# Copying mask factors on GpSimd, turning inputs earlier and moving two transform steps to another PSUM bank, in a fused block-sparse attention and Fourier-mixing kernel

## The chip, the cores and the metric

The kernel runs on one core of a Trainium2 chip. The metric is the device time of one execution in microseconds (us), lower is better. All times below are medians of runs in the fast state. Engines are written PE (TensorE, matrix products), PEld (its weight loads), DVE (VectorE), ACT (ScalarE), POOL (GpSimd) and SP (SyncE, which issues DMAs). "L580" is line 580 of the kernel.

## The reference, cut to what matters

Attention over 4 batches and 8 heads with a block mask, then a Fourier mixing block with a channel network. All is float32.

```python
# q, k, v: (4, 8, 768, 64); blocks of 32; mask: neighbours, first and last block, 3 random blocks a row
scores = scale * q @ k^T;  scores = where(mask, scores, -1e9)
attn = softmax(scores);    o = attn @ v
x = o.transpose(0, 2, 1, 3).reshape(4, 768, 512)
mixed = real(fft(fft(x, axis=1), axis=2))
u = x + mixed
un = (u - mean(u)) / sqrt(var(u) + 1e-6)            # "whitened"
out = u + relu(un @ w_ch1) @ w_ch2                  # 512 -> 2048 -> 512
```

## The kernel before

Two heads of one batch make a pair; there are 16 pairs. A pair has 6 slots, so a batch has SB = 24, and a slot computes the scores, exponentials and values of 2 units (128 keys by 384 queries for both heads). The Fourier and channel work of one batch, its "mixer", is woven in behind the attention of the next batch. The weaving is done while the kernel is built: each engine has a modelled clock `when`, each PSUM bank a modelled time `free`, and `gap` emits mixer work while the model says that it fits. On the chip every engine then works through its own list in that fixed order, so the place of an instruction in the list matters as much as its duration.

Some names of tiles: `s` and `e` are scores and their exponentials; `oT` and `xt` carry the output of the attention into `x`. The others in the profiles belong to the mixer: `sa` and `sd` to its folds (sums and differences of rows before the transform), `zp` and `zs` to the transform's later steps, `un`, `utp` and `unT` to the whitened tiles, and `xp`, `yp`, `z` and `y` are its products.

The mask of the first batches can be added by the matrix unit, through two bf16 factors (L580). They lie in buffers that later serve the running sums of the exponentials, so they are copied away in slot 19:

```python
    def keep_factors():                                    # called when sl == SB - 5
        kept = room(2, [P, 2, S], "factors", BF16)         # the room of a weight chunk
        for a, t in enumerate(factors["at"]):
            nc.sync.dma_start(out=kept[:, a, :], in_=t)    # L479
        factors["at"] = kept[:, 0, :], kept[:, 1, :]       # all later units read the copy
```

From the fifth pair on, keys and queries of the next pair are turned by VectorE in blocks of 32 (`flip_blocks`, L537) and put in order by ScalarE (`in_order`, L545); `squares` takes a sum of squares for a range check. The order within a slot, cut:

```python
        got = scores(units)                                # PE: L570, and L580 for the mask
        for u, ps in got:
            weigh(u, ps)                                   # ACT: exponential; DVE: mask, where PE didn't add it
        if not paired and not late:
            gap(1.5)                                       # mixer work that fits, such as the folds
        while due and (opens or not paired):
            sum_up()                                       # values (PE L633), and sums (DVE L614 or POOL L619)
        ...                                                # more mixer work, channel steps, copies
        if BY_VECTOR <= n + 1 < len(pairs):                # the turns, at the end of the slot
            for at, fn, args in ((0, squares, (n + 1, 0)), (1, flip_blocks, (n + 1, 0)),
                                 (2, in_order, (n + 1,)), (4, flip_blocks, (n + 1, 1)),
                                 (5, squares, (n + 1, 1))):
                if s == at:
                    fn(*args)
```

The sums of a pair close in `total`, which reads both halves of the summed exponentials, `acc`, and frees their buffers:

```python
    def total(n):
        sp, at = ps_t.tile([P, HS], FP32, tag="t", name="sp"), bank("t")
        for half in range(2):
            acc = acc_of.pop((n, half))
            for i in range(2):
                ...
                nc.tensor.matmul(sp[g:g + BLK, :], ..., acc[:, i, :], ...)      # L715
```

PSUM has one bank "t" and two banks "m" for small steps. The third step of the transform, `along(2)`, took both "m" banks (`side` and `zp`), and the last whitened tile was turned over (`un_flip(1, 1)`, L958) through an "m" bank. An "m" bank is also where the products of the mixer want to go.

## Time and profile before

| | before |
|---|---|
| median (lowest to highest) | 1080.43 (1079.89 to 1081.24), 4 runs |
| span of the profiled execution | 1079.5 |
| PE busy | 1042.1 |
| PE idle | 37.4 |
| longest waits of PE | 9.2 for the copied factors, 4.5 for the turned keys |

A line of the timeline has the start, the time taken, the engine, the kernel's line, the operation, the output and the inputs with their shapes, and a count when equal instructions were put together; the bracket at the end is idle time of that engine just before, and who ended it. The prediction shows the main lines. These, from the timeline of the kernel before, matter later. They are two of the last folds in VectorE's list before the sum at 166.66, and the next sum of GpSimd:

```profile
165.65 0.56 DVE L788 TENSOR_TENSOR sa<-sa 128x384 f32<-128x384 f32 x1
166.13 0.29 DVE L787 TENSOR_TENSOR e<-e 128x128 f32<-128x128 f32 x1
...
171.43 1.00 POOL L619 TENSOR_TENSOR acc<-e 128x384 f32<-128x384 f32 x1 [7.69 <-ACT e L590]
```

GpSimd starts the next pair's sums at 171.43, a microsecond after L715 has begun at 170.42, and so after the folds.

### The profile page before, as it was taken

Reading aid. Unit: us, or ns where it says so; the run is one execution under the profiler, and the core shown is the slowest. Engines: PE = TensorE matmul, PEld = TensorE weight load, DVE = VectorE, ACT = ScalarE, POOL = GpSimd, SP = SyncE. Lnnn points to the kernel's source line nnn. Section 1 sums busy time; section 2 is a strip of 40 time slices with the busy share of each in tenths; the row PEclk is TensorE's granted clock in tenths of the full one; section 3 lists DMA queues with packets and bytes.
Section 4 is the critical chain, followed back from the end, with each engine's and each line's share of the span. In section 5 each row is a group of like instructions: output and inputs, shape, how many; then the busy total and the mean of one; then the engine's idle time right before and its main releaser. Section 6 shows DMA issues by size and latency. Waiting matters only on the chain.

```text
span 1079.5 us, 12378 instructions
## 1 busy us (share of the span) xinstructions
PE 1042.1 (97%) x4378; PEld 537.1 (50%) x4378; DVE 661.5 (61%) x1226; ACT 376.4 (35%) x742; POOL 227.4 (21%) x256
## 2 busy tenths in 40 slices
PE   8999789999999999999999999999999999999996
PEld 4433234444455545444444555444444555568575
DVE  5899494777763634764568446665557255675663
ACT  5998555564311202443451302343320212210210
POOL 1000062323600001265454000354630001000000
PEclk9999899999999999999999999999999999999998
DMA  7757222221000001222211000212000001000001
GB/s 224 220 177 239 69 45 44 45 45 30 15 0 1 1 0 30 59 39 42 52 29 31 1 0 18 64 29 39 14 9 7 0 1 30 29 1 1 1 19 43
DMA packets 120769, 47.04 MB, mean 44 GB/s; under 512 B 108142, under 2 KB 113532, under 8 KB 120700
## 3 DMA queue, kind: packets, MB, share of 16 engines
q1 hardware_dynamic: 118812, 45.38, 17.1%
q10 hardware_dynamic: 1856, 0.79, 0.3%
q8 instruction: 36, 0.59, 0.2%
q14 instruction: 33, 0.27, 0.1%
q0 software_dynamic: 32, 0.01, 0.0%
HBM read 37.11 MB, written 6.29 MB: 40 GB/s over the span
## 4 chain that ended last, share of the span: by engine, by line
PE 90%; DVE 6%; issue 2%; ACT 1%; DMA 0%; POOL 0%; SPq 0%; ACTq 0%; POOLq 0%; DVEq 0%
PE y L1089 23%; PE z L1033 15%; PE s L570 12%; PE o L633 11%; PE yp L1033 8%; PE yy L1152 6%; PE xp L1033 4%; PE zp L843 2%; PE sp L701 1%; PE s L580 1%; PE zp L814 1%; PE tp L503 1%; PE utp L958 1%; PE sp L715 1%; PE xt L657 1%
## 5 line engine op out<-in xcount | busy, mean ns | idle before, releaser
L619 POOL TENSOR_TENSOR acc<-acc,e 128x384 f32<-128x384 f32 x154 | 156.8, 1055 | 212.2 <-ACT e L590 137.6
L570 PE MATMUL s<-qT,kT 64*128 64x384 f32 x768 | 154.3, 517 | 7.7 <-DVE kT L537 4.5
L633 PE MATMUL o<-e,vr 128*64 128x384 f32 x768 | 142.8, 500 | 0.0
L1092 DVE TENSOR_TENSOR x<-y,x 128x512 f32<-128x512 f32 x72 | 49.7, 690 | 133.1 <-PE y L1089 133.0
L1089 PE MATMUL y<-w_sb,hA 128*128 128x512 f32 x288 | 129.3, 596 | 1.7 <-ACT zs L845 1.7
L1089 PE MATMUL y<-w_sb,hB 128*128 128x512 f32 x288 | 128.5, 596 | 1.0 <-DVE x L1092 1.0
L595 DVE TENSOR_TENSOR e<-s,mask 128x768 f32<-128x768 f32 x98 | 89.0, 950 | 54.2 <-ACT s L593 48.5
L570 PEld LDWEIGHTS s<-qT,kT 64*128 64x128 f32 x768 | 64.6, 187 | 82.8 <-issue 26.1
L593 ACT ACTIVATE s<-s 128x768 f32<-128x768 f32 x98 | 74.3, 791 | 84.2 <-PE s L570 83.9
L1033 PE MATMUL z<-unT,t 128*128 128x384 f32 x256 | 93.2, 487 | 0.3 <-DVE hA L1038 0.3
L1089 PEld LDWEIGHTS y<-w_sb,hB 128*128 128x128 f32 x288 | 53.4, 190 | 67.7 <-issue 65.3
L590 ACT ACTIVATE e<-s 128x768 f32<-128x768 f32 x94 | 71.2, 812 | 42.6 <-PE s L580 38.6
L1089 PEld LDWEIGHTS y<-w_sb,hA 128*128 128x128 f32 x288 | 53.0, 190 | 65.5 <-issue 58.8
L906 POOL TENSOR_SCALAR st<-st 128x1 f32<-128x1 f32 x24 | 8.3, 348 | 358.8 <-DVE st L905 358.8
L633 PEld LDWEIGHTS o<-e,vr 128*64 128x64 f32 x768 | 48.3, 137 | 71.0 <-issue 67.6
L1038 DVE TENSOR_TENSOR hA<-z,hA 128x384 f32<-128x384 f32 x64 | 35.7, 557 | 77.8 <-PE z L1033 77.8
L1042 ACT ACTIVATE hA<-hA 128x384 f32<-128x384 f32 x64 | 33.4, 523 | 120.4 <-DVE hA L1038 120.3
L619 POOL TENSOR_TENSOR acc<-e 128x384 f32<-128x384 f32 x40 | 42.9, 1094 | 111.9 <-PE sp L715 85.7
L1033 PEld LDWEIGHTS z<-unT,t 128*128 128x128 f32 x256 | 48.5, 190 | 34.7 <-DVE hA L1038 1.3
L1042 ACT ACTIVATE hB<-hB 128x384 f32<-128x384 f32 x64 | 33.5, 523 | 85.9 <-DVE hB L1038 85.9
L1053 ACT COPY hA<-xp 128x384 f32<-128x384 f32 x32 | 15.3, 479 | 113.0 <-PE xp L1033 113.0
L1033 PE MATMUL xp<-unT,w_sb 128*128 128x384 f32 x128 | 47.6, 494 | 2.6 <-DVE x L1092 2.6
(204 smaller groups left out, 1430.8 us busy)
## 6 DMA issues: line engine op xcount, KB each, us to landing
wraw<-in_moe_w_ch_dram SPq DMA_DIRECT2D x32, 512.0 KB
vr<-in_v_dram SPq DMA_DIRECT2D x30, 192.0 KB
qb<-in_q_dram SPq DMA_DIRECT2D x44, 96.0 KB
kb<-in_k_dram SPq DMA_DIRECT2D x44, 96.0 KB
x<-oT SPq DMA_DIRECT2D x192, 12.0 KB
out_dram<-x SPq DMA_DIRECT2D x16, 128.0 KB
out_dram<-x SPq DMA_DIRECT2D x8, 256.0 KB
qr<-in_q_dram SPq DMA_DIRECT2D x24, 64.0 KB
```

Source lines behind the costliest of these rows:

```text
L570: nc.tensor.matmul(s[:, i, 0:HS], kT[rows, c * P:(c + 1) * P], qT[rows, queries], start=True, stop=u not in by_pe)
L590: nc.scalar.activation(out=e, in_=s[:, :, 0:HS], func=ACT.Exp, scale=scale)
L593: nc.scalar.activation(out=s[:, :, 0:HS], in_=s[:, :, 0:HS], func=ACT.Exp, scale=scale)
L595: nc.vector.tensor_tensor(out=e, in0=s[:, :, 0:HS], in1=m.broadcast_to([P, 2, HS]), op=ALU.mult)
L619: nc.gpsimd.tensor_add(out=acc[:, i, :], in0=start[:, i, :], in1=e[:, i, :])
L633: nc.tensor.matmul(o[D * i:D * i + D, :], vt[:, i, c, :], e[:, i, :], start=(c == 0), stop=(c == C - 1))
L1033: nc.tensor.matmul(to, a[:, k, :], c[:, k, :], start=(k == 0), stop=(k == ND // 2 - 1))
L1038: tt(out=to, in0=ps, in1=a, op=ALU.add)
L1042: nc.scalar.activation(out=h, in_=h, func=ACT.Relu)
L1089: nc.tensor.matmul(y, hs[0, half][:, l, m * P:(m + 1) * P], w2_sb[:, 4 * r + l, :], start=(l == 0), stop=(l == 3))
L1092: nc.vector.tensor_tensor(out=x[:, m, :], in0=y, in1=x[:, m, :], op=ALU.add)
L1152: nc.tensor.matmul(ps, a[:, k, :], c[k // 2][:, k % 2, :] if isinstance(c, list) else c[:, k, :], start=(k == 0), stop=(k == 3))
```

## The change

It has three intentions: GpSimd copies the factors in place of two DMAs; the turns stand right behind the exponentials of their slot, so that the turned keys are there earlier; the transform's third step and the last whitened tile use the turns' bank "t", so that an "m" bank is left for products. The diff without its bookkeeping for the model:

```diff
-            nc.sync.dma_start(out=kept[:, a, :], in_=t)
+            nc.gpsimd.tensor_copy(out=kept[:, a, :], in_=t)
...
-                side = ps_m.tile([P, 512], FP32, tag="m", name="side")
-                at = bank("m")
+                side, at = ps_t.tile([P, 512], FP32, tag="t", name="side"), bank("t")
...
-        first += [("M" if g == 2 else "m", lambda g=g: along(g), 2.1, (1.0 if g < 2 else 0.5), 0.0)
+        first += [("mt" if g == 2 else "m", lambda g=g: along(g), 2.1, (1.0 if g < 2 else 0.5), 0.0)
...
-            tag, pool = (("t", ps_t), ("m", ps_m))[half]
+            tag, pool = (("t", ps_t), ("m", ps_m))[half == 1 and m != 1]
...
         for u, ps in got:
             weigh(u, ps)
+        if BY_VECTOR <= n + 1 < len(pairs):
+            for at, fn, args in ((0, squares, (n + 1, 0)), (1, flip_blocks, (n + 1, 0)),
+                                 (2, in_order, (n + 1,)), (4, flip_blocks, (n + 1, 1)),
+                                 (5, squares, (n + 1, 1))):
+                if s == at:
+                    fn(*args)
         if not paired and not late:
             gap(1.5)
...
-        if BY_VECTOR <= n + 1 < len(pairs):
-            ...                                   (the same lines, at the end of the slot)
```

I call the three parts A (the copy), B (the turns) and C (the banks).

More of the change, by code (lines that the diff above doesn't have):

```diff
@@ L1194, in outputs @@
             ahead(4)
-        fl = [[("tm"[h], lambda h=h, m=m: un_flip(h, m), 0.6, 0.55, 0.0) for m in range(T)]
+        fl = [[("tm"[h == 1 and m != 1], lambda h=h, m=m: un_flip(h, m), 0.6, 0.55, 0.0)
+               for m in range(T)]
               for h in range(2)]
@@ L1252, in do_apart @@
         if kind != "-":
-            at = bank(kind.lower())
+            at = bank(kind[0])
             done = busy("PE", pe, done) + HOP
@@ L1279, in gap @@
             elif kind != "-":
-                bank_at = (max if kind == "M" else min)(free[kind.lower()])
-                if kind.lower() in used or max(state["ready"], bank_at) > when["PE"] + 0.1:
+                bank_at = max(min(free[k]) for k in kind)
+                if (any(k in used for k in kind) or
+                        max(state["ready"], bank_at) > when["PE"] + 0.1):
                     break
-                used += kind.lower()
+                used += kind
             do_apart()
@@ L1444, in slot @@
             item[2]()
-        if BY_VECTOR <= n + 1 < len(pairs):
-            for at, fn, args in ((0, squares, (n + 1, 0)), (1, flip_blocks, (n + 1, 0)),
-                                 (2, in_order, (n + 1,)), (4, flip_blocks, (n + 1, 1)),
-                                 (5, squares, (n + 1, 1))):
-                if s == at:
-                    fn(*args)
         w_loads()
```

## The prediction

> **What bounds the kernel now.** I read the page first, then the list of waits of TensorE, then the timeline around the long ones, then a table of stretches for the clock. To order the timeline by the program I also had the unchanged program print the order in which it emits its work; no time comes from that.
>
> The page and the waits of TensorE (who waited for whom, us in total, times, longest):
>
> ```profile
> span 1079.5 us, 12378 instructions
> PE 1042.1 (97%) x4378; PEld 537.1 (50%) x4378; DVE 661.5 (61%) x1226; ACT 376.4 (35%) x742; POOL 227.4 (21%) x256
> ...
> PE s L580 <- DMA factors<-at_q: 9.2, 1, 9.2
> PE s L570 <- DVE kT L537: 4.5, 1, 4.5
> ...
> PE xp L1033 <- DVE x L1092: 2.6, 3, 1.8
> PE y L1089 <- ACT zs L845: 1.7, 3, 0.6
> PE s L570 <- DVE e L595: 1.6, 2, 0.8
> ```
>
> TensorE is busy 97%, so only its idle time, 1079.5 - 1042.1 = 37.4 us, and any time at a low clock can be won. The change adds no matmul and takes none away. The five waits shown are 19.6 of the 37.4 us, and each of the three parts of the change aims at some of them.
>
> The timeline at the first wait (start, duration, engine, line):
>
> ```profile
> 110.17 0.69 DVE L462 TENSOR_TENSOR w_sb<-w_sb,wraw 128x512 f32<-128x512 f32 x1
> 110.92 0.53 SPq L479 DMA_DIRECT2D factors<-at_k  x1
> 111.50 0.60 SPq L479 DMA_DIRECT2D factors<-at_q  x1
> ...
> 115.64 0.82 PE L580 MATMUL s<-factors 64*128 64x384 bf16 x4 [9.16 <-DMA factors<-at_q]
> ```
>
> The copies can't start before 110.86, when VectorE has finished with the weight chunk in whose buffer the copy goes (110.17 + 0.69). The transfer is only the last 115.64 - 110.86 = 4.8 us of the 9.16; the rest is that buffer.
>
> At the second wait:
>
> ```profile
> 154.10 2.54 DVE L766 TENSOR_TENSOR sa<-x 128x1536 f32<-128x1536 f32 x1
> ...
> 160.71 1.49 DVE L537 STREAM_TRANSPOSE kT<-kb 128x768 f32<-128x768 f32 x1
> ...
> 162.35 2.93 PE L570 MATMUL s<-qT,kT 64*128 64x384 f32 x8 [4.53 <-DVE kT L537]
> ...
> 166.66 0.95 DVE L614 TENSOR_TENSOR acc<-acc,e 128x768 f32<-128x768 f32 x1
> ...
> 170.42 0.85 PE L715 MATMUL sp<-acc,pick 128*32 128x384 f32 x8
> ```
>
> The turn of the keys stands behind three folds in VectorE's queue (at 154.10, 156.57 and 159.05), and VectorE has no gap from 147.09 to 168.75. Eight score matmuls that take 1.5 us elsewhere took 2.93 here. The table of stretches (us, PE busy and count, the other engines, granted clock, DMA share, GB/s) says why:
>
> ```profile
> 115.60:120.50 4.90, 4.86 (x20) 1.10 (x19) 0.00 (x0) 1.51 (x2) 0.00 (x0) 0.50 0.00 0
> ...
> 162.30:165.00 2.70, 2.65 (x8) 1.47 (x10) 2.66 (x4) 0.87 (x2) 1.43 (x2) 0.50 0.26 42
> ```
>
> After both long waits the clock is halved: 4.86 us of work behind the first and 2.65 behind the second cost half of that, 2.4 and 1.3 us. So the first wait costs 9.2 + 2.4 = 11.6, the second 4.5 + 1.3 = 5.8 us.
>
> **What the Trainium skill says.**
> - "TensorE: Matmul & The Clock Gate", "What's actually happening": an idle window of about 3.4 us halves the clock, and a busy one of the same length restores it. The trace agrees: both low stretches follow idle times over 3.4 us, and no shorter wait has one.
> - "GPSIMD Engine Reference", "4.1 Engine selection": one-input operations run near line rate on GpSimd, two-input ones about twice as slow as on VectorE; "3.1 Elementwise" gives about 2.6 cycles an element for two inputs and 1.03 to 1.8 for short loops. The kernel has no GpSimd copy; its additions of 384 columns take 1055 ns in the mean, 0.98 when undisturbed, which agrees with 2.6 cycles.
> - "DMA: Bandwidth & Descriptors", "Anatomy of one DMA": some 2 us fixed plus the size over the bandwidth, so about 2.5 us for 192 KB. Here the second transfer took 4.1 us from its issue (111.50) to its use (115.64): slower, behind earlier loads.
> - "SBUF — State Buffer", "SBUF: two separate sides": VectorE instructions with two SBUF inputs and GpSimd exclude each other. It agrees: L614 takes 1.76 us at 152.42 beside GpSimd's sums and 0.95 alone. The new copies run at 110.9, when VectorE is idle until 123.8, so they meet nobody.
>
> **Part 1, the copy by GpSimd.** Removed: two DMAs. Added: two one-input copies of 128x768. Estimate from the GPSIMD page: 768 x 1.03 to 1.8 cycles at 1.2 GHz is 0.66 to 1.15 us, plus some 0.15 us each, so 1.6 to 2.6 us for both, which start at 110.9 as the DMAs do. TensorE goes on at 112.6 to 113.6, I take 113.0: 2.6 us earlier. The idle time is still 6.5 us, so the clock still falls. With the low windows where they lie now (steps of 3.41 us, one ending at 117.1, the next at 120.5) the low stretch is 113.0 to 117.1 in place of 115.6 to 120.5: 0.4 us less loss. Gain 3.0 us. From there to 147 no other wait of TensorE is over 0.4 us, so it is kept.
>
> **Part 2, the turns.** Nothing is added or removed; the turn of the keys moves in front of the three folds that the same slot emits. It then runs from about 154.2 to 155.7 (its data landed before 144, by the DMA packets), and TensorE needs it at 157.8. Taken alone this wins the whole 5.8 us. But the sum of VectorE's work up to L614 at 166.66 is the same, and that addition closes the sums that L715 reads. TensorE stands in order: scores of the slot from 157.85, next slot's scores, values up to about 165, then L715, which can't start before 167.61 + 0.1. Now it starts at 170.42. So I keep 2.7 us, and about 2.7 us of new idle time appear in front of L715. That is shorter than a window, so I count no lower clock. Further, squaring the keys now comes directly behind the exponentials of its own slot and no longer holds up the exponentials of the next one, which is what the timeline shows before the 0.78 us wait at 258.88: 0.7 us. In all other slots the order on ScalarE and VectorE hardly changes. Gain 3.4 us.
>
> **Part 3, the banks.** The transform's third step took both "m" banks, and the next y product waited for a copy out of one (0.57 us, three times): 1.7 us gained. The last whitened tile leaves its "m" bank, so the first product of the next quad need not wait for L1092. But two of these three waits won't vanish: at 444 and 694 the "t" bank holds the softmax sums, which VectorE takes out at 444.75 and 696.01, when L1092 is nearly done as well. So only the last (0.35 us) counts, and I subtract 0.5 us for a stall on "t" behind the sums. Gain 1.5 us.
>
> Sum: 3.0 + 3.4 + 1.5 = 7.9 us; 1080.5 - 7.9 = 1072.6.
>
> **Rivals.**
> (a) VectorE's chain does not bind and the turn's whole cost is won: another 3 us, 1069.5. For it: the order of folds and sums may change, since the emission follows a model of busy times. Against: VectorE has no gap from 147 to 168.75.
> (b) The new wait in front of L715 is long enough to halve the clock, and GpSimd's copy is slow (2 us each, as two-input ones would be): the first part wins about 1 us and the second about 1.5: some 1076.
> (c) The earlier turns and the shared "t" bank disturb the later batches, where exponentials, masks and quads stand close: each lost 0.5 us, in three batches, some 1075. Against it: in paired slots the turn was emitted close behind the exponentials already.
> (d) The buffer of the weight chunk comes free later because something else on VectorE comes first. Against: nothing before 110 changes.
>
> **Range and chances.** I predict 1072.5 us. Part 1 may be 1 us off either way, part 2 from 1 to 6, part 3 from -1 to 3; together some 4 us each way: 1068.5 to 1077. Two per cent are 21.6 us; all waits that the change can reach, with their clock loss, are 11.6 + 5.8 + 5.9 = 23.3 us, so faster by over 2% needs nearly all of them gone: 1%. Slower by over 2% would need a new wait of 22 us: 1%.
>
> **What would show it.** Step 1: two GpSimd copies of 0.8 to 1.3 us from 110.9, the wait at L580 about 6.5 us, still a low clock behind it. Step 2: no wait of scores for kT; a wait of some 2.7 us in front of L715 for L614, near 162 to 165. Step 3: no wait of y for zs. It is wrong if the copies take over 2 us, if TensorE does not wait at L715 and the time falls below 1069, or if a wait for exponentials, masks or the "t" bank grows by over 2 us.

## The result, and the profile after

| | before | after |
|---|---|---|
| median (lowest to highest), 4 runs each | 1080.43 (1079.89 to 1081.24) | 1077.72 (1076.34 to 1078.51) |
| ratio, with its 95% interval | | 0.9973 (0.9956 to 0.9990) |
| span of the profiled execution | 1079.5 | 1075.9 |

A ratio is the mean time of one kernel's fast runs over that of the other's fast runs of the same rounds, so it isn't quite the ratio of the medians. By the rule of 2% the kernels are the same. The gain is 2.7 us where I had predicted 7.9, and the time lies 0.7 us above my range.

The page of the kernel after:

```profile
span 1075.9 us, 12388 instructions
...
PE 1042.7 (97%) x4378; PEld 536.5 (50%) x4378; DVE 665.4 (62%) x1226; ACT 375.7 (35%) x742; POOL 231.1 (21%) x258
```

PE's idle time fell from 37.4 to 33.2 us, and its busy time grew by 0.6 us although it has the same 4378 products. So some of them ran longer; a table below shows where the clock was lower. The waits of PE after (who waited for whom; us in total, times, longest):

```profile
PE s L580 <- POOL factors L479: 6.1, 1, 6.1
PE sp L715 <- DVE acc L614: 3.8, 1, 3.8
...
PE xt L657 <- ACT unT L958: 2.0, 1, 2.0
```

The wait for the factors shrank from 9.2 to 6.1, the waits for turned keys (4.5) and for `zs` (1.7) are gone, and the two longest new ones are at L715 and L657. To see what each stretch gained I set the start of the same slot's first score product against itself in both traces:

| slots | after minus before, us | what is there |
|---|---|---|
| 0 to 20 | -0.3 | nothing changed: scatter |
| 20 to 22 | -3.4 | the factors |
| 22 to 30 | -4.0 | the wait for turned keys (-4.5), a new one of 0.5 |
| 30 to 36 | +6.0 | the new wait at L715 (3.8), and more work at a low clock behind it than before |
| 36 to 42 | 0.0 | |
| 42 to 54 | +1.5 | the new wait at L657, less what the banks gain there |
| 54 to 60 | +0.5 | the banks: two new waits, 0.2 and 0.5, for one of 0.4 |
| 60 to 84 | -1.6 | the banks |
| 84 to the last product | -1.8 | the banks |
| behind the last product | -0.5 | |

The sum is -3.6, the difference of the spans. Three of these rows deserve their lines. First the factors, in the timeline after:

```profile
110.68 0.82 POOL L479 COPY factors<-at_k 128x768 bf16<-128x768 bf16 x1 [105.58 <-DVE w_sb L462]
111.45 0.83 POOL L479 COPY factors<-at_q 128x768 bf16<-128x768 bf16 x1
112.33 0.82 PE L580 MATMUL s<-factors 64*128 64x384 bf16 x4 [6.15 <-POOL factors L479]
```

GpSimd had nothing to do for 105.58 us; it waited for VectorE to leave the weight chunk in whose room the copy goes. Both copies together are over in 1.6 us, but the wait is still 6.15 us, because most of it is that room.

Then the sums, about 50 us later, in the timeline after:

```profile
150.96 1.54 DVE L537 STREAM_TRANSPOSE kT<-kb 128x768 f32<-128x768 f32 x1
...
161.33 0.84 PE L715 MATMUL sp<-acc,pick 128*32 128x384 f32 x4
162.34 2.27 POOL L619 TENSOR_TENSOR acc<-e 128x384 f32<-128x384 f32 x2 [1.73 <-ACT e L590]
162.53 1.23 DVE L788 TENSOR_TENSOR sa<-sa 128x384 f32<-128x384 f32 x1
163.69 1.08 DVE L787 TENSOR_TENSOR e<-e 128x128 f32<-128x128 f32 x1
...
165.01 0.95 DVE L614 TENSOR_TENSOR acc<-acc,e 128x768 f32<-128x768 f32 x1
166.01 1.50 PE L715 MATMUL sp<-acc,pick 128*32 128x384 f32 x4 [3.84 <-DVE acc L614]
```

Read it from the bottom. The second half of L715 waited 3.84 us for the sum of 165.01. That sum is late because two folds before it took 1.23 and 1.08 us, where they took 0.56 and 0.29 before. They took longer because GpSimd's sum lies right beside them, from 162.34. And that sum could start because the first half of L715 had run at 161.33 and given back its buffer: before, all eight products of L715 came together, after the folds. (The bracket of GpSimd's sum names the exponentials, which came last; that it needs the buffer too is shown by e4.)

The table of stretches after (start:end, us, then PE, PEld, DVE, ACT and POOL busy with counts, granted clock, DMA share, GB/s) shows what the new wait does to the clock:

```profile
161.40:164.80 3.40, 0.77 (x5) 0.07 (x4) 3.33 (x5) 0.06 (x1) 2.27 (x2) 0.99 0.00 0
164.80:171.50 6.70, 5.49 (x17) 2.19 (x18) 5.40 (x9) 1.50 (x2) 0.00 (x0) 0.50 0.01 2
```

PE worked 5.49 us at half the clock there; if half of it is loss, that is 2.7 us. In the kernel before, PE worked 3.18 us at half the clock behind the wait for turned keys (162.12 to 165.53), by the same estimate a loss of 1.6 us.

Last the wait at L657, in the timeline after:

```profile
230.86 1.88 ACT L545 COPY qT<-qb 128x256 f32<-128x256 f32 x6
232.65 0.58 ACT L958 COPY unT<-utp 128x512 f32<-128x512 f32 x1
233.28 0.55 PE L657 MATMUL xt<-ident,oT 128*128 128x128 f32 x3 [1.99 <-ACT unT L958]
```

and the same step of the kernel before:

```profile
232.68 0.59 ACT L959 COPY unT<-utp 128x512 f32<-128x512 f32 x1
233.15 1.92 ACT L545 COPY qT<-qb 128x256 f32<-128x256 f32 x6
```

The two ScalarE entries have changed places. The copy to `unT` empties bank "t", of which there is only one, and L657 needs that bank; so six small copies of `in_order`, 1.88 us, now stand between PE and its bank.

### The profile page after: what moved, and what is told of

It reads as the page before. It is cut to its first block, busy times and chain, and to the rows that moved or that the text cites. A ratio compares the mean times of both kernels' runs of the same rounds, so it can differ in the third digit from the quotient of the medians.

```text
span 1075.9 us, 12388 instructions
## 1 busy us (share of the span) xinstructions
PE 1042.7 (97%) x4378; PEld 536.5 (50%) x4378; DVE 665.4 (62%) x1226; ACT 375.7 (35%) x742; POOL 231.1 (21%) x258
## 4 chain that ended last, share of the span: by engine, by line
PE 88%; DVE 7%; ACT 2%; issue 2%; POOL 1%; DMA 0%; ACTq 0%; DVEq 0%; POOLq 0%
PE y L1088 22%; PE z L1032 15%; PE s L570 12%; PE o L633 10%; PE yp L1032 7%; PE yy L1151 6%; PE xp L1032 4%; PE zp L842 2%; PE sp L701 1%; PE s L580 1%; PE zp L814 1%; PE utp L957 1%; DVE x L743 1%; PE sp L715 1%; PE tp L503 1%
## 5 line engine op out<-in xcount | busy, mean ns | idle before, releaser
L619 POOL TENSOR_TENSOR acc<-acc,e 128x384 f32<-128x384 f32 x150 | 152.1, 1050 | 85.3 <-DVE e L595 83.2
L619 POOL TENSOR_TENSOR acc<-e 128x384 f32<-128x384 f32 x44 | 48.2, 1115 | 127.1 <-PE sp L715 93.6
L1032 PE MATMUL z<-t,w_sb 128*128 128x384 f32 x128 | 46.7, 488 | 0.9 <-DVE t L994 0.9
```

The source lines that it names most:

```text
L619: nc.gpsimd.tensor_add(out=acc[:, i, :], in0=start[:, i, :], in1=e[:, i, :])
L1032: nc.tensor.matmul(to, a[:, k, :], c[:, k, :], start=(k == 0), stop=(k == ND // 2 - 1))
```

## The experiments

**My theory.** A does what I predicted. B removes the wait for keys, but gives that back at L715, where the chain of VectorE also gets longer through the collision with GpSimd and the clock halves; and it loses some 2 us more by `in_order` in front of the copy that empties bank "t". C gains more than I had counted. **The rivals.** (1) The parts disturb each other, and none of them alone loses. (2) The loss after slot 42 belongs to C, which puts more work through bank "t". (3) The long wait at L715 is merely VectorE's sum of work, and the collision has no part in it.

All twelve runs gave correct results, in the fast state. They came in three calls, on three chips, and each is given as a ratio to the kernel before on the same chip, whose medians were 1080.89, 1080.67 and 1080.65 us. All ratios lie within 2% of 1, so all of them are "same" by that rule; the intervals tell them apart.

### e1: the copy alone

The kernel before, with A:

```diff
-            nc.sync.dma_start(out=kept[:, a, :], in_=t)
+            nc.gpsimd.tensor_copy(out=kept[:, a, :], in_=t)
```

> The kernel before with the GpSimd copy alone. Theory (the ledger of the two traces): the wait for the factors goes from 9.2 to 6.1 us and the low clock behind it from some 4.9 to some 4 us of work, 3.4 us in all, and nothing else changes: 1077.1 us, the wait for kT stays at 4.5 us. Rival: an earlier first stage is eaten by the chain of VectorE before kT, whose wait then grows: 1080, wait for kT over 6 us.

Measured: 1077.63 us (1076.85 to 1078.02, 6 runs), ratio 0.9969 (0.9956 to 0.9981), which is 3.3 us gained. The wait for the factors is 6.2 us and the wait for keys still 4.5. The theory holds for A.

### e2: the turns alone

The kernel before, with the block of five turn steps moved to behind `weigh`, as in the change.

> The kernel before with the earlier turns alone. Theory: the wait for kT (4.5 us and 1.3 us of low clock) is replaced by a wait of 3.8 us in front of L715, longer than a clock window of 3.4 us, so the clock is halved again and some 2.8 us are lost: no gain, 1080 to 1083 us. Rival (my prediction's second step): the wait in front of L715 is 2.7 us, without a low clock behind it: 1077 us.

Measured: 1084.35 us (1083.64 to 1085.25, 6 runs), ratio 1.0033 (1.0020 to 1.0045): 3.5 us lost, more than I had expected, since that left out L657. Its waits of PE:

```profile
PE sp L715 <- DVE acc L614: 3.8, 1, 3.8
...
PE xt L657 <- ACT unT L959: 2.0, 1, 2.0
```

Both new waits are there without A and C. The clock was 0.50 from 166.0 to 172.8, as long as after the whole change. Rival 1 falls: a part that I had credited with 3.4 us costs 3.5.

### e3: the banks alone

The kernel before, with C.

> The kernel before with the two changes of banks alone. Theory: the waits of y for zs (1.7 us) and of xp for L1092 (2.6 us) go, two short ones on the t bank and for L994 come (0.7 each), so 2.8 us are won after 430 us: 1077.7 us if the 1.5 us that the changed kernel lost between 221 and 430 us belong to the turns, 1079.2 us if they belong to the banks (a new wait of L657 for L958 near 233 us would show it). Rival (prediction's third step): 1.5 us won, 1079.

Measured: 1076.48 us (1075.19 to 1078.25, 5 runs), ratio 0.9959 (0.9945 to 0.9973): 4.4 us gained, where I had expected 3.2, or 1.7 if the wait at L657 belonged to the banks. The waits for `zs` (1.7 us) and for `un` at the products `yp` (0.5) are gone; the three waits of `xp`, 2.6 us, are replaced by 0.5 at L957 (bank "t"), 1.0 at the products `z` and 0.35 at a product `y`. Two of these in its list of waits:

```profile
PE z L1032 <- DVE t L994: 1.0, 2, 0.5
...
PE utp L957 <- DVE sums L683: 0.5, 2, 0.2
```

From slot 36 to the last product PE's idle time is 3.0 us less and the time 4.1 us less. There is no wait at L657, and slots 42 to 54, which lost 2.3 us in e2, gain 1.3 us here. Rival 2 falls.

### e4: the halves of the total reversed

The kernel after, with the late half of L715 first, so that no buffer comes free before the folds are over:

```diff
-        for half in range(2):
+        for half in (1, 0):
```

> The changed kernel with the two halves of the sum in L715 in reversed order: its first four matmuls then wait for L614, so the sums' first buffer stays taken and GpSimd can't start the next pair's sums at 162.3 us, beside VectorE's folds. Theory: L788 and L787 go back from 1.23 and 1.08 us to 0.56 and 0.29, L614 ends 1.5 us earlier, the wait in front of L715 is 2.4 to 2.9 us (four matmuls more stand behind it), under a clock window, and no low clock follows: 1074 to 1075 us. Rival: the wait grew from 2.7 to 3.8 us because the turn of the keys or a different order made VectorE's chain longer; then the wait stays near 3.8 to 4.3 us with the low clock: 1077.5 to 1078.5 us.

Measured: 1075.59 us (1073.94 to 1075.81, 5 runs), ratio 0.9947 (0.9933 to 0.9960), 2.8 us better than the change. Its timeline:

```profile
162.64 0.56 DVE L788 TENSOR_TENSOR sa<-sa 128x384 f32<-128x384 f32 x1
163.11 0.28 DVE L787 TENSOR_TENSOR e<-e 128x128 f32<-128x128 f32 x1
163.64 0.95 DVE L614 TENSOR_TENSOR acc<-acc,e 128x768 f32<-128x768 f32 x1
164.65 1.36 PE L715 MATMUL sp<-acc,pick 128*32 128x384 f32 x8 [3.14 <-DVE acc L614]
166.15 2.18 POOL L619 TENSOR_TENSOR acc<-e 128x384 f32<-128x384 f32 x2 [5.42 <-PE sp L715]
```

The folds are back at 0.56 and 0.28 us, and the last sum starts at 163.64 instead of 165.01, 1.4 us earlier. Rival 3 falls: the collision cost that much. In slots 30 to 36 this kernel needs 2.4 us less than the change. The wait gives 0.7 of them. The other 1.7 us are PE's busy time: 3.41 us of work at half clock in place of 5.54, and the eight products of L715 together in 1.36 us, where the two separate halves took 0.84 and 1.50. Yet I missed two things. The wait is 3.14 us where I had expected 2.4 to 2.9, since the early half of L715 no longer fills a part of it. And I had expected no low clock behind it, but one of 3.4 us came, although the wait was shorter than a step of the clock. What makes the clock fall was thus open; e7, e9 and e10 bear on it.

### e5: the copy and the banks, without the turns

> The changed kernel without the earlier turns (copy and banks). Theory: the parts add up (3.3 for the copy, 4.4 for the banks, -3.5 for the turns in the runs of them alone), so this is faster than the changed kernel: 1073.2 us, with the kT wait of 4.5 us still in it. Rival: the parts overlap, and without the turns the changed kernel loses: 1077 to 1080 us.

Measured: 1074.47 us (1073.17 to 1075.17, 5 runs), ratio 0.9941 (0.9928 to 0.9955), a gain of 6.2 us. Against the change's 0.9973 that is 3.5 us better: B costs the same beside A and C as alone. A and C together are 1.5 us less than 3.3 + 4.4 us, within the intervals of the two. The traces show where such scatter can come from: behind the unchanged wait for keys the low clock lasted 6.8 us here and 3.4 us before, because the steps of the clock fell otherwise.

### e6: the turn of the keys alone

The kernel before, with only the turn of the keys moved:

```diff
         for u, ps in got:
             weigh(u, ps)
+        if BY_VECTOR <= n + 1 < len(pairs) and s == 4:
+            flip_blocks(n + 1, 1)
...
-                                 (2, in_order, (n + 1,)), (4, flip_blocks, (n + 1, 1)),
-                                 (5, squares, (n + 1, 1))):
+                                 (2, in_order, (n + 1,)), (5, squares, (n + 1, 1))):
```

> The kernel before with one of the five moved steps alone, the turn of the keys; squares, the queries' turn and its ordering stay at the end of the slot. Theory: the swap of the kT wait for the L715 wait (3.3 to 3.8 us and a low clock of up to 6.8 us) is here, so it gains nothing: 1081 to 1082.5 us; but the 2.3 us that the turns alone lost between 221 and 430 us are not, since they come from the ordering of the queries (1.9 us on ScalarE) queued in front of the copy L959 that frees the t bank. So it is 2 to 3 us faster than the turns alone (1084.35), and no wait of L657 for L959 is seen. Rival: the loss after 221 us comes from the keys' turn or from the model's busy times; then 1083.5 to 1085 and the wait of 2.0 us is there.

Measured: 1081.37 us (1080.62 to 1082.05, 13 runs), ratio 1.0006 (0.9998 to 1.0014). The wait for keys is gone, the wait at L715 is 3.86 us with a low clock of 6.8 us behind it, and no wait is left at L657. So this step, the one that was worth the trouble, gave everything back at the next wait (the interval includes no change at all), and the other moved steps cost the remaining 1.0033 - 1.0006 = 0.0027, that is 2.9 us.

### e7: A, C and the keys' turn, with the sums in front of the folds

To A, C and the step of e6 I added the reversed halves of e4, and in slot 30, the one whose sum closes the pair, the mixer's folds come after the sums:

```diff
-        if not paired and not late:
+        if not paired and not late and sl not in (30,):
             gap(1.5)
         while due and (opens or not paired):
             sum_up()
+        if not paired and not late and sl in (30,):
+            gap(1.5)
```

> Copy, banks and the keys' turn alone, the halves of L715 reversed, and in the one slot after the turn the sums (L614) emitted in front of the last folds. Theory: VectorE's chain up to the last sum is what TensorE waits for at L715; with about 1.7 us of folds behind it the wait falls to 1 to 2 us and no low clock follows: 1068.5 to 1071 us. Rival: another wait, for example of the third step L814 for the folds, takes its place at the same size: 1072 to 1074 us.

Measured: 1070.58 us (1069.39 to 1071.77, 4 runs), ratio 0.9902 (0.9887 to 0.9917). The time is inside what I expected, but the wait is not: 2.55 us instead of 1 to 2, with the clock at half again. Its table of stretches:

```profile
158.40:161.80 3.40, 1.25 (x10) 0.50 (x8) 3.26 (x6) 1.87 (x4) 0.00 (x0) 1.00 0.45 127
161.80:165.20 3.40, 3.00 (x14) 0.99 (x16) 3.30 (x7) 0.91 (x2) 1.36 (x2) 0.50 0.03 5
```

PE was busy for 1.25 of the 3.4 us, and the clock halved all the same.

### e8: the copy by GpSimd, three slots later

A alone left a wait of 6.2 us, most of which is for the room of the weight chunk. So I let the units of three more slots read the original factors:

```diff
-        if sl == SB - 5:
+        if sl == SB - 2:
             keep_factors()
```

> The kernel before with the GpSimd copy, issued three slots later (slot 22 of 24), when the weight chunk has long left the buffer. Theory: 4.5 of the 6.1 us that remain at L580 are the wait for that buffer and only 1.65 the copies, which then run beside TensorE's work: the wait and the low clock behind it vanish (6.1 + 2 us): 1069 to 1070.5 us. Rival: VectorE and ScalarE, which idle during the wait, become the bound with their weight rounds and take part of it: 1072 to 1075 us.

Measured: 1070.03 us (1069.63 to 1070.77, 4 runs), ratio 0.9901 (0.9886 to 0.9916): 10.6 us gained over the kernel before, and 7.3 more than A alone. Its timeline:

```profile
109.97 0.82 POOL L479 COPY factors<-at_k 128x768 bf16<-128x768 bf16 x1 [104.87 <-DVE w_sb L462]
110.73 0.83 POOL L479 COPY factors<-at_q 128x768 bf16<-128x768 bf16 x1
...
114.23 0.49 PE L580 MATMUL s<-at_q,at_k 64*128 64x384 bf16 x4
```

The copies run at the same time as in the kernel after, 110 us, as soon as the room is free. But PE, at 114.23, still reads `at_q` and `at_k`, the originals, and has stopped for nothing; its first use of the copy comes at 119.22. The wait at L580 and the low clock behind it are gone. What is new is a wait of 1.2 us for exponentials. Whether the two DMAs, with their first use as late, would have done as well was not run: in the kernel before they took 4.8 us from the moment the room was free, and here 9 us lie between the start of the copies and their first use.

### e9: e7 with the later copy

> The kernel of the keys' turn with the sums first (1070.58 us), with the copy three slots later. Theory: the two waits are independent, so the 7.6 us that the later copy won over the early one come on top: 1063 us (1062 to 1064.5). Rival: with TensorE 7.6 us earlier, VectorE's weight rounds or loads of the keys hold up the turn: 1065 to 1068 us.

Measured: 1063.66 us (1062.92 to 1063.93, 5 runs), ratio 0.9845 (0.9831 to 0.9858). The gains of e7 and e8 add up to 0.0098 + 0.0099 = 0.0197; the two share A (0.0031), which leaves 0.0166, and 0.0155 came. The wait at L715 is 2.17 us, and the clock halved once more, from 153.15 to 156.56.

### e10: e9 with the folds held back in two slots

```diff
-        if not paired and not late and sl not in (30,):
+        if not paired and not late and sl not in (29, 30):
```

Only slot 30 calls `gap` again behind its sums; in slot 29 the folds are left to the later calls.

> As e9, and in two slots in place of one the sums go in front of the folds, so one more fold (L770 of sd, 0.95 us) stands behind the last sum. Theory: the wait in front of L715 falls from 2.5 to some 1.6 us, and the window that halves the clock is then more than half busy: 1 to 2.5 us faster than e9: 1060.5 to 1062 us. Rival: the sums wait for GpSimd or for the exponentials instead: within 0.5 us of e9.

Measured: 1062.17 us (1062.06 to 1062.46, 5 runs), ratio 0.9832 (0.9818 to 0.9845). Its page and its timeline at L715:

```profile
PE 1036.4 (98%) x4378; PEld 535.4 (51%) x4378; DVE 662.8 (63%) x1225; ACT 376.1 (35%) x742; POOL 227.5 (21%) x260
```

```profile
152.99 0.85 PE L715 MATMUL sp<-acc,pick 128*32 128x384 f32 x8 [1.17 <-DVE acc L614]
```

The time is 0.2 us above what I had expected. A wait of 1.17 us is left (in a step of the clock with PE busy for 2.25 us), and the clock is nowhere at half before the last product: PE's busy time for the same 4378 products is 1036.4 us, 5.7 us less than before. This is the best version, 1080.65 - 1062.17 = 18.5 us faster than the kernel before; against the change the ratios differ by 0.9973 - 0.9832 = 0.0141, some 15 us.

### e11: e8 with the banks, the turns unmoved

> Copy three slots later and the banks, with the turns where they were. Theory: 1074.5 - 7.6 = 1066.9 us, with the kT wait of 4.5 us and its low clock; what e9 is faster by (about 4 us) is then what the keys' turn is worth once the sums don't wait. Rival: the turn is worth nothing in any order: same as e9.

Measured: 1066.39 us (1065.59 to 1067.10, 4 runs), ratio 0.9872 (0.9857 to 0.9887). Its wait for keys is 4.5 us. Against e9 and e10 it shows what the earlier turn of the keys is worth together with the reversed halves and the held-back folds: 2.7 and 4.2 us. What those two would win without the turn was not run; e11 has no wait at L715 that they could shorten. The idea of turning the keys earlier was good; its surroundings took the gain.

### e12: the turns moved, except `in_order`

The kernel before, with four of the five steps moved and `in_order` left at the end of the slot:

```diff
+            for at, fn, args in ((0, squares, (n + 1, 0)), (1, flip_blocks, (n + 1, 0)),
+                                 (4, flip_blocks, (n + 1, 1)),
+                                 (5, squares, (n + 1, 1))):
...
+        if BY_VECTOR <= n + 1 < len(pairs) and s == 2:
+            in_order(n + 1)
         w_loads()
```

> All turns earlier, as in the run of the turns alone (1084.35), but the ordering of the queries stays at the end of its slot. Theory: the 2.0 us wait of L657 for the copy L959 comes from those 1.9 us on ScalarE in front of L959; it goes, and with it 1.5 to 2.5 us: 1082 to 1083 us. Rival: the wait comes from the changed order of TensorE's program that the earlier turns bring about through the model's busy times, and remains: 1084 to 1085 us.

Measured: 1082.26 us (1080.78 to 1083.38, 19 runs), ratio 1.0013 (1.0007 to 1.0020), so 0.0020 or 2.1 us better than e2 (the two intervals just touch). The wait at L657 shrank from 2.0 to 0.7 us, and slots 42 to 54 lose 0.2 us instead of 2.3. Gone, too, is a wait of 1.0 us for exponentials that e2 and the change have in slot 53. `in_order` was the cause of most of the second loss.

## Why the prediction was wrong

| part | predicted gain, us | measured alone, us |
|---|---|---|
| A, the copy | 3.0 | 3.3 (e1) |
| B, the turns | 3.4 | -3.5 (e2) |
| C, the banks | 1.5 | 4.4 (e3) |
| sum | 7.9 | 4.2; the whole change 2.7, within the scatter that e5 shows |

**Part 1 was right**, by its own steps: two copies of 0.82 and 0.83 us from 110.68, a wait of 6.15 us, a low clock still behind it. That the gain fits so well is partly luck. The wait shrank by 3.0 us, where I had 2.6; the 0.4 us for a shorter low clock can't be credited to the copy. PE worked 3.6 to 5.5 us at half clock behind this wait in the five traces with the DMAs (before, e2, e3, e6, e12), and 4.1 to 4.9 in the five with the early GpSimd copy. I had also read both low stretches as too short: by the records of the clock they end at 121.16 and 165.53, not at 120.5 and 165.0, with 5.52 and 3.18 us of work in them, not 4.86 and 2.65. What I left unsaid was the better question. I had written that only 4.8 of the 9.16 us are the transfer and the rest is the buffer, and then worked out how much a faster copy wins. e8 shows that the copy's speed was not the point: with the originals read for three slots more, the whole wait goes, and the low clock with it.

**Part 2 is the step that failed**, in this sentence: "So I keep 2.7 us, and about 2.7 us of new idle time appear in front of L715. That is shorter than a window, so I count no lower clock." The place was right, both of its numbers were not.

- The wait was 3.84 us. I took the sum of VectorE's work up to L614 as fixed. From the first L743 to the end of the last sum it was 20.52 us before (147.09 to 167.61) and 22.04 after (143.92 to 165.96). Moving the keys let the first half of L715 run ahead, that freed a buffer, and GpSimd's next sums ran into VectorE's folds. The prediction itself had named this exclusion, and asked only whether the new copies would meet it. e4 took the collision away and won 1.4 us at L614.
- The clock did fall, for 6.8 us. "Shorter than a window" was the wrong test. The step of 3.41 us that ended at 164.73 had PE busy for 0.86 us, so it was not idle, and the clock halved at its end. e4, e7 and e9, with waits of 3.14, 2.55 and 2.17 us, show the same; e10, with 1.17 us, does not. I named a halved clock at L715 in rival (b), and dismissed it by that test. Rival (b)'s other half, a slow copy, did not happen.
- "In all other slots the order on ScalarE and VectorE hardly changes" was wrong too, in slots 42 to 54, where `in_order` came in front of the copy that empties bank "t". e12 puts 2.1 us on it. That is rival (c) in one of its three batches, with its size far above the 0.5 us I gave it. The 0.7 us that I credited for earlier squares came where I had put them: the wait of 0.78 us at 258.88, in slot 49, is gone in the change, in e2 and in e12. But with `in_order` moved, in the change and in e2, scores wait 1.02 us for masked exponentials in slot 53 instead (289.55 after); in e12 they don't.

By the runs, B is made of the keys' turn (0.0006, 0.7 us lost: 4.5 us of wait and some 1.6 of clock won; 3.9 of wait and, with 5.95 us of work at half clock, some 3.0 lost again), of `in_order` (2.1 us lost), and of the rest (1.0013 against 1.0006, 0.7 us, among it a wait of 0.5 us for the copy of `oT`, behind the moved squares).

**Part 3 had the mechanism right and the size wrong.** The term that was mis-sized is "So only the last (0.35 us) counts": I held that two of the three waits of `xp` would stay because bank "t" is in use then. In e3 these three waits of 2.6 us gave way to others of 0.5 + 1.0 + 0.35 = 1.85 us, which is 0.75 us won where I had 0.35 less 0.5. The longest of the three, 1.82 us, became one of 0.24 for bank "t": I had taken the time at which VectorE empties that bank as fixed, but in e3 it came 4.1 us after the start of L715 (687.81 to 691.93), and before 5.5 us after it (689.91 to 695.46). The waits for `un` at `yp`, 0.5 us, I had not counted at all; the 1.7 us for `zs` came as predicted. Together that is 3.0 us less idle time. The time fell by 4.1 us over the same slots, and the other 1.1 us is a shorter busy time of PE for the same products (866.2 to 865.1). I had no term for that at all. Why it is shorter is not shown: eight products `y` behind a wait for `zs` took 3.70 us before and 3.60 at the same place in e3, but others took 3.70 with no wait in front of them (at 436.45 before).

Had I sized C right and kept my error on B, I should have predicted 1080.5 - 3.0 - 3.4 - 4.4 = 1069.7 and missed by 8 us; so the two errors partly cancelled, by luck.

**What makes the clock fall**, as far as the traces show it. From the records of products and of the granted clock, each low stretch in the table begins at the end of a step of 3.41 us:

| kernel, place | wait, us | PE busy in the step before, of 3.41 | low clock after it |
|---|---|---|---|
| before, keys | 4.53 | 0.00 | 3.4 us |
| after, L715 | 3.84 | 0.86 | 6.8 us |
| e4, L715 | 3.14 | 0.27 | 3.4 us |
| e7, L715 | 2.55 | 1.29 | 3.4 us |
| e9, L715 | 2.17 | 1.39 | 3.4 us |
| before, `xp` at 696.65 | 1.82 | 1.59 | none |
| after, L657 | 1.99 | 1.71 | none |
| before, step from 104.09, in which the factors' wait begins | the first 1.0 of 9.16 | 2.38 | none |

The same holds for all steps of the 14 kept traces: at full clock, every step with PE busy for 1.39 us or less was followed by half the clock, and none with 1.56 us or more. How long the low clock lasts follows from the next step: after the change it was 2.13 us busy and the clock stayed low, in e7 it was 2.99 us and the clock came back; over all traces, 2.53 us or less kept it low and 2.81 us or more brought it back. The exact limits between these numbers stay open, and the busy times rest on ends of products that the profiler models. Nor do the steps stand still: from one run to the next they fall otherwise, as e5 showed. So a wait of about two microseconds costs either nothing or half of the next step's work, by where it falls: the 1.99 us at L657 after the change cost no clock, the 2.17 us in e9 did. e10, in which no step is low before the last product, has a range of 0.4 us over its runs, the change 2.2 us.

## What to carry to other kernels

Before you credit a removed wait, follow the same engine's list to the next thing that must close, and ask which buffer an earlier instruction gives back and who starts work on it; here that was GpSimd beside VectorE's folds, and it cost as much as was won. Before you make a copy faster, ask whether its readers have to wait for it at all: letting them read the original three slots longer, with the faster copy, won 10.6 us, where the faster copy alone won 3.3. Before you move a small step forward on an engine, look whether it comes in front of a copy that empties a PSUM bank of which there is only one; here that cost 2 us.

## What the Trainium skill lacked or had wrong

- "TensorE: Matmul & The Clock Gate", "What's actually happening": it has the clock halve after an idle window of some 3.4 us. Neither this page nor another says how busy a window may be and still count as idle. Here windows in which PE was busy for 0.86, 1.29 and 1.39 us of 3.41 did it too, and waits of 2.55 and 2.17 us were enough; in the 14 traces no window with 1.56 us or more did. For the way back, 2.53 us busy was too little and 2.81 enough.
- "GPSIMD Engine Reference", "4.1 Engine selection": one-input operations near line rate held, but no page has a figure for a GpSimd copy in bf16. Here 128x768 took 0.82 and 0.83 us, 1.07 ns a column, with VectorE idle; the two-input additions of the same kernel took 1055 ns for 384 columns, 2.7 ns a column.
